# Key loading in 768-byte pieces and key turning by half-width identity products, in a fused attention and feed-forward kernel

## The chip, the cores and the metric

The kernel runs on one core of one Trainium2 chip (trn2). The metric is the device time of one execution in microseconds (us), as the median of several runs. Engine names: PE is TensorE's matrix product, PEld its weight load, ACT is ScalarE, DVE is VectorE, POOL is GpSimd, SP is SyncE, which here only issues DMAs. ACTq and SPq are the instruction queues of ACT and SP, where DMAs are issued.

## The reference

Attention with mixed heads, then a feed-forward layer. Batch 4, 12 heads, 448 positions, head size 64; the feed-forward sizes are 768 and 2048.

```python
scores = scale * np.matmul(q, k.transpose(0, 1, 3, 2))
scores = np.einsum('bhij,hg->bgij', scores, w_pre)
scores = scores - np.max(scores, axis=-1, keepdims=True)
attn = np.exp(scores)
attn = attn / (np.sum(attn, axis=-1, keepdims=True) + 1e-09)
attn = np.einsum('bhij,hg->bgij', attn, w_post)
attn_out = np.matmul(attn, v)
x = attn_out.transpose(0, 2, 1, 3).reshape(B * S, H * D)
h = x @ w_in
g = np.where(h >= 1, h, np.where(h <= -1, 0.0, (h + 1) ** 2 / 4))
return g @ w_out
```

## The kernel before, in words

The program has two halves. The first (about the first 465 us) is the attention, the second the feed-forward layer; only the attention is touched.

The attention goes through 16 tiles of query rows, four for each element of the batch (120, 120, 120 and 88 rows), all 12 heads at once. Each tile is cut into 3 groups, 48 groups in all, and each group holds 3 or 4 blocks: a block has up to 10 query rows times 12 heads, 120 partitions by 448 key positions.

Heads go in pairs, six pairs to an element of the batch. For a pair the keys must lie with the head dimension on the partitions: two heads of 64 fill 128 partitions. `load_k` (L101) brings the keys of a pair into SBUF with the key positions on the partitions; `trans_k` (L136) turns them on PE. Of the 448 positions of a head, 384 go as three blocks of 128 (L141), the last 64 by a product of their own (`rest`, L149). ACT copies the turned keys out of PSUM as the high part (L145), DVE makes the low part (L146). `trans_q` (L153) does the same for the queries of a tile, in two halves of three pairs (L161, L165, L166). `scores` (L169) takes two pairs: three products for each head (high by high, high by low, low by high, L180), copies out by DVE (L185 or L187) and ACT (L189) into `ssb`. With `ring` false the first pair lies in one wide PSUM tile, which DVE copies at once (L187); with `ring` true in two tiles of the ring of six banks `ps_l`, copied one by one (L185). In both cases ACT copies the two heads of the second pair.

Both `load_k` and the tile it fills put the two heads of a pair side by side, so one transpose turns both:

```python
x = x.rearrange("p (r s d) -> p r s d", s=2, d=D)
for s in range(2):
    e.dma_start(out=x[:, :, s, :], in_=k[b, 2 * hp + s, :SM].rearrange("(p r) d -> p r d", r=KC))
```

In DRAM the three rows `r` of a partition are 768 contiguous bytes; in the tile they lie apart, so the transfer moves pieces of 256 bytes.

From `ssb` each block is fetched again by DMA with rows and heads on the partitions (`load_s`, L202, tile `s`), mixed over heads on PE (`pre`, L221 and L223), maximum on DVE (L226), exponential on ACT (L232), the second mix on PE (`post`, L260, and `post_rest`, L276), and the product with the values on PE (`pv`, L306 and L311). `post` and `pv` write 64 PSUM partitions at a time: products with 64 columns of weights that go to one or the other column half of PE, two at once.

The order is written by hand (`manual_schedule`): every engine works through its instructions in program order, and a waiting instruction holds what stands behind it. The main loop (L893) issues for group n, on PE: `pre` of its blocks, the turning of the next element's keys and of the next tile's queries where they are due, `pv`, `post_rest` and `post` of the group before, then `scores` of the next tile. The keys of the next element are turned in three consecutive groups, two pairs in each, so in 9 groups over the whole program; they are fetched one group earlier. DMA issues go through the queues of SP and, for some keys of the first tile, of ACT. Completion semaphores are used in turn, so a DMA's issue can also wait until the DMA that had its semaphore before has landed.

The first tile has code of its own (L758 to L823). It loads the queries (L762, L767, L770) and the first element's keys (L766 to L769) into three tiles `k0`, which later become those of the values; builds the identity on POOL; issues products of the identity with itself, whose result nobody reads (`warm`, L788), so that PE has work while the first data come; turns queries and keys, makes the scores in three steps of two pairs, loads the values, fetches the first blocks, and goes on to the second tile's scores.

Of the kernel before, what the change touches and what calls it, by code (L numbers as in the profile page):

```python
# [22 lines left out]
def tile_talking_heads_moe(  # L23
# [76 lines left out]

    def load_k(b, hp, t=None):  # L101
        e = nc.scalar if t is not None and hp > 2 else nc.sync
        if t is None:
            t = qp.tile([128, 2 * S // 128 * D + D], F32, tag="kraw", name="kraw", bufs=2)
            x, y = t[:, :2 * KC * D], t[:KR, 2 * KC * D:]
            i = ident[:KR, :KR]
        else:
            j = hp % 2
            x, y = t[:, 2 * KC * D * j:2 * KC * D * (j + 1)], t[j * KR:(j + 1) * KR, 4 * KC * D:]
            i = ident[j * KR:(j + 1) * KR, j * KR:(j + 1) * KR]  # L110
        x = x.rearrange("p (r s d) -> p r s d", s=2, d=D)
        y = y.rearrange("p (s d) -> p s d", d=D)
        for s in range(2):
            e.dma_start(out=x[:, :, s, :], in_=k[b, 2 * hp + s, :SM].rearrange("(p r) d -> p r d", r=KC))
        e.dma_start(out=y, in_=k[b, 2 * hp:2 * hp + 2, SM:].rearrange("s p d -> p s d"))
        kraw[b, hp] = x, y, i

# [8 lines left out]
    def load_v(b, g):  # L126
        t = ap_.tile([128, 4 * KC * D + 2 * D], F32, tag=f"v{g}", name=f"v{g}", bufs=1)
        x = t[:, :4 * KC * D].rearrange("p (h c) -> p h c", h=4)
        y = t[:, 4 * KC * D:].rearrange("p (s d) -> p s d", d=D)
        nc.sync.dma_start(out=x, in_=v[b, 4 * g:4 * g + 4, :SM].rearrange("h (p r) d -> p h (r d)", r=KC))  # L130
        for m in range(2):
            h = 4 * g + 2 * m
            nc.sync.dma_start(out=y[half[m]], in_=v[b, h:h + 2, SM:].rearrange("s p d -> p s d"))
        vt[b, g] = x, y

    def trans_k(b, hp):  # L136
        kt[b, hp] = [qp.tile([128, S], F32R, tag=f"k{c}{hp}", name=f"k{c}{hp}", bufs=1) for c in "hl"]
        x, y, i = kraw.pop((b, hp))
        ps = ps_l.tile([128, S], F32, tag="l", name="ps_k")
        for r in range(KC):  # L140
            nc.tensor.transpose(out=ps[:, r * 128:(r + 1) * 128], in_=x[:, r, :, :], identity=ident)  # L141

        def out():
            hi, lo = kt[b, hp]
            nc.scalar.activation(out=hi, in_=ps, func=AF.Copy)  # L145
            nc.vector.tensor_tensor(out=lo, in0=ps, in1=hi.bitcast(F32), op=ALU.subtract)  # L146

        def rest():
            nc.tensor.transpose(out=ps[:, SM:], in_=y, identity=i)  # L149
            return out  # L150
        return rest
# [17 lines left out]
    def scores(t, hps, ring=False):  # L169
# [13 lines left out]
        if ring:  # L183
            for s in range(2):
                nc.vector.tensor_copy(out=ssb[t][:n, h + s, :], in_=ps[0][s][:n])  # L185
        else:
            nc.vector.tensor_copy(out=ssb[t][:n, h:h + 2, :], in_=wide[:n, :, :S])  # L187
        for s in range(2):
            nc.scalar.activation(out=ssb[t][:n, 2 * hps[1] + s, :], in_=ps[1][s][:n], func=AF.Copy)  # L189

# [567 lines left out]
    with tc.manual_schedule():  # L758
# [6 lines left out]
        ident = qp.tile([128, 128], F32, name="ident", bufs=1)  # L765
        load_k(0, 0, k0[0])  # L766
        load_q(0, (1,))  # L767
        for hp in range(1, HP):
            load_k(0, hp, k0[hp // 2])  # L769
        load_q(1)  # L770
# [18 lines left out]

        warm(12)  # L790
        trans_q(0, 0)()()
        trans_k(0, 0)()()
        warm(3)
        trans_q(0, 1)()()
        warm(4)
        trans_k(0, 1)()()
        for g in range(3):
            scores(0, [2 * g, 2 * g + 1], g == 1)
            if g < 2:
# [311 lines left out]
```

## Time and profile before

| what | value |
|---|---|
| median of 3 runs | 873.71 us (872.88 to 875.06) |
| profiled execution, its own time | 873.89 us |
| its span, first to last instruction | 872.2 us |
| PE busy | 855.1 us, 98% of the span |
| DVE, ACT, POOL busy | 644.0, 563.0, 212.7 us |
| mean granted clock of PE | 0.998 |

The span is the stretch that the profile's rows cover; 1.7 us of the execution's own time lie outside it. A row of the timeline gives start, length, engine, line, operation, what it writes and reads, the shape and how many such instructions follow one another. PE's instructions overlap: a single one is in the pipeline for some 270 ns, though the next may start 110 ns later, so the time that a run of them costs is read from start to start. A float32 product stands as two records, a transpose as one. The chain of waits is followed back from the last instruction to whatever released it.

### The profile page before, as it was taken

How to read it: one execution, taken by the hardware profiler on the slowest of the kernel's cores; microseconds unless marked ns; L12 is line 12 of the kernel's file. 1: busy time of each engine (PE TensorE's matmuls, PEld its weight loads, DVE VectorE, ACT ScalarE, POOL GpSimd, SP SyncE). 2: the span in 40 equal slices, each digit the busy share in tenths (PEclk: the TensorE clock that was granted, in tenths of full speed). 3: DMA queues.
4: the chain of work that ended last, by engine and by line, in shares of the span. 5: the costliest groups of instructions: out<-in, count | busy, mean ns of one | idle time of the engine just before them, and what ended most of it. 6: DMA issues, size and time to landing. Idle time of an engine off the chain costs nothing.

```text
span 872.2 us, 19952 instructions
## 1 busy us (share of the span) xinstructions
PE 855.1 (98%) x7848; PEld 735.8 (84%) x7848; DVE 644.0 (74%) x938; ACT 563.0 (65%) x1171; POOL 212.7 (24%) x269
## 2 busy tenths in 40 slices
PE   8999999999999999999999999999999999999998
PEld 6678777777777787777778788899999999999998
DVE  3887587775767866768578977997668978777853
ACT  3788788787877777778666466676667434433431
POOL 0366245662455633656320000000000000000000
PEclk9999999999999999999999999999999999999999
DMA  7887769987689875997556755664434544123331
GB/s 161 238 250 216 220 192 258 276 238 217 180 248 263 252 212 154 277 269 254 189 171 171 250 180 175 208 188 128 127 109 163 174 153 136 55 90 111 108 128 63
DMA packets 155329, 162.47 MB, mean 186 GB/s; under 512 B 66916, under 2 KB 148964, under 8 KB 155236
## 3 DMA queue, kind: packets, MB, share of 16 engines
q1 hardware_dynamic: 152404, 160.51, 61.1%
q8 instruction: 62, 1.02, 0.5%
q10 hardware_dynamic: 2832, 0.69, 0.4%
q14 instruction: 31, 0.25, 0.1%
HBM read 88.81 MB, written 33.82 MB: 141 GB/s over the span
## 4 chain that ended last, share of the span: by engine, by line
PE 83%; DMA 6%; DVE 4%; ACT 4%; SPq 2%; issue 1%; POOL 0%; ACTq 0%; DVEq 0%; POOLq 0%
PE ps_f L712 23%; PE ps_f L547 21%; PE ps_a L260 10%; PE ps_l L223 7%; DMA s<-ssb 5%; PE ps_q L311 5%; PE ps_l L221 4%; PE ps_q L180 3%; PE ps_s L180 3%; PE ps_r L276 2%; PE ps_q L306 1%; ACT e L232 1%; PE ps_t L161 1%; SPq L202 1%; PE ps_k L141 1%
## 5 line engine op out<-in xcount | busy, mean ns | idle before, releaser
L243 POOL TENSOR_SCALAR wr<-wpost,rs 120x120 f32<-120x120 f32 x180 | 140.3, 795 | 62.5 <-DVE rs L239 43.2
L232 ACT ACTIVATE e<-ps_l,nm 120x448 f32<-120x448 f32 x180 | 112.2, 631 | 63.1 <-DVE nm L226 61.8
L260 PE MATMUL ps_a<-wr,e 120*64 120x120 f32 (+1 forms) x2160 | 118.9, 266 | 0.0
L226 DVE TENSOR_REDUCE nm<-ps_l 120x1 f32<-120x448 f32 x180 | 105.0, 617 | 14.3 <-PE ps_l L223 10.8
L260 PEld LDWEIGHTS ps_a<-wr,e 120*64 120x64 f32 x2160 | 110.2, 137 | 2.6 <-issue 2.6
L695 ACT ACTIVATE sgh_p<-gq_p 128x1024 fp32r<-128x1024 f32 (+1 forms) x56 | 53.3, 953 | 89.9 <-PE ps_f L712 89.7
L223 PE MATMUL ps_l<-s,wpre 120*120 120x448 f32 x196 | 94.8, 568 | 5.7 <-DMA s<-ssb 3.4
L439 DVE SCALAR_TENSOR_TENSOR wl<-wi,wh 128x768 fp32r<-128x768 f32 x71 | 67.7, 953 | 41.9 <-ACT wh L436 41.9
L712 PE MATMUL ps_f<-wh,sgh_p 128*128 128x384 f32 x294 | 98.2, 334 | 0.0
L712 PE MATMUL ps_f<-wh,sgl_p 128*128 128x384 f32 x294 | 98.2, 334 | 0.0
L712 PE MATMUL ps_f<-wl,sgh_p 128*128 128x384 f32 x294 | 98.2, 334 | 0.0
L436 ACT ACTIVATE wh<-wi 128x768 fp32r<-128x768 f32 x71 | 59.7, 842 | 58.0 <-DVE wi L659 18.0
L262 ACT ACTIVATE aT<-ps_a 128x360 f32<-128x360 f32 x180 | 79.4, 498 | 12.9 <-PE ps_a L260 4.7
L696 DVE TENSOR_TENSOR sgl_p<-gq_p,sgh_p 128x1024 fp32r<-128x1024 f32 (+1 forms) x56 | 60.8, 1088 | 35.8 <-ACT sgh_p L695 35.8
L210 DVE CAST sh<-s 120x448 fp32r<-120x448 f32 (+1 forms) x82 | 32.9, 401 | 59.2 <-DMA s<-ssb 59.0
L187 DVE COPY ssb<-ps_q 120x896 f32<-120x896 f32 (+1 forms) x46 | 49.9, 1084 | 26.9 <-PE ps_q L180 26.8
L189 ACT ACTIVATE ssb<-ps_s 120x448 f32<-120x448 f32 (+1 forms) x96 | 47.5, 554 | 20.7 <-PE ps_s L180 17.6
L377 POOL TENSOR_TENSOR wt<-wt,wk 128x768 int32<-128x768 int32 x32 | 58.2, 1820 | 8.9 <-ACT wk L373 5.8
L221 PE MATMUL ps_l<-sh,wpre_h 120*120 120x448 f32 (+1 forms) x82 | 59.6, 726 | 0.0
L712 PEld LDWEIGHTS ps_f<-wh,sgh_p 128*128 128x128 f32 x294 | 55.2, 188 | 0.0
L712 PEld LDWEIGHTS ps_f<-wl,sgh_p 128*128 128x128 f32 x294 | 55.2, 188 | 0.0
L712 PEld LDWEIGHTS ps_f<-wh,sgl_p 128*128 128x128 f32 x294 | 55.2, 188 | 0.0
(235 smaller groups left out, 1949.4 us busy)
## 6 DMA issues: line engine op xcount, KB each, us to landing
s<-ssb SPq DMA_DIRECT2D x172, 210.0 KB
wraw<-in_moe_w_in_dram SPq DMA_DIRECT2D x16, 768.0 KB
wraw<-in_moe_w_out_dram SPq DMA_DIRECT2D x16, 768.0 KB
wi<-wod SPq DMA_DIRECT2D x29, 384.0 KB
wi<-wsd SPq DMA_DIRECT2D x28, 384.0 KB
wsd<-wt SPq DMA_DIRECT2D x16, 384.0 KB
wod<-wt SPq DMA_DIRECT2D x16, 384.0 KB
wi<-wss SPq DMA_DIRECT2D x16, 384.0 KB
```

The source lines that it names most:

```text
L221: nc.tensor.matmul(out=lps[m], lhsT=w[:k], rhs=y[:k], start=(j == 0), stop=(j == 2))
L223: nc.tensor.matmul(out=lps[m], lhsT=wpre[:k], rhs=x[:k], start=True, stop=True)
L226: nc.vector.tensor_reduce(out=nm, in_=lps[m], axis=AX.X, op=ALU.max, negate=True)
L232: nc.scalar.activation(out=e, in_=ps, func=AF.Exp, bias=nm, accum_out=sm[:, j:j + 1])
L243: nc.gpsimd.tensor_scalar_mul(out=w[:, :, :ni], in0=wpost[:, :, :ni], scalar1=rs[:, j:j + 1])
L260: nc.tensor.matmul(out=ps[half[s], r, :ni * H], lhsT=e[:, c0:c0 + 64], rhs=w[:, :, :ni], start=True, stop=True)
L262: nc.scalar.activation(out=a[:, :, :, c:c + ni], in_=ps[:, :, :ni * H].rearrange("q r (h i) -> q r h i", h=H), func=AF.Copy)
L436: nc.scalar.activation(out=hi, in_=t, func=AF.Copy, scale=2.0 ** -8)
L439: nc.vector.scalar_tensor_tensor(out=lo, in0=t, scalar=2.0 ** -8, in1=hi.bitcast(F32), op0=ALU.mult, op1=ALU.subtract)
L547: nc.tensor.matmul(out=o, lhsT=u[:, c, k], rhs=x, start=first and r == 0 and m == 0, stop=r == 2 and m == 2, skip_group_check=True)
L696: nc.vector.tensor_tensor(out=lo, in0=src, in1=hi.bitcast(F32), op=ALU.subtract)
L712: nc.tensor.matmul(out=o, lhsT=x[:, f, c], rhs=y[:, f % 2, :], start=first and f == 0 and m == 0, stop=hf == 1 and f == 3 and m == 2, skip ...
```

## The change

The keys of a pair, or of four heads in the first tile, are now loaded by one DMA whose pieces are 768 bytes, with the heads one after the other in the tile. A 128-column block of weights with both heads is then no longer contiguous, and `trans_k` makes two products of 64 columns with the identity instead of one transpose, one for each head, into the two partition halves of PSUM. In the first tile the loads are regrouped (one DMA for four heads; the 64-position rests of the first four pairs on ACT's queue, all else on SP's), there are 8 of the unread products instead of 19, the second pair's keys are turned before the second half of the queries, and all steps but the first use the ring. In ring steps DVE now copies the first head of both pairs and ACT the second head of both.

```diff
-    def load_k(b, hp, t=None):
-        e = nc.scalar if t is not None and hp > 2 else nc.sync
...
-        x = x.rearrange("p (r s d) -> p r s d", s=2, d=D)
-        y = y.rearrange("p (s d) -> p s d", d=D)
-        for s in range(2):
-            e.dma_start(out=x[:, :, s, :], in_=k[b, 2 * hp + s, :SM].rearrange("(p r) d -> p r d", r=KC))
-        e.dma_start(out=y, in_=k[b, 2 * hp:2 * hp + 2, SM:].rearrange("s p d -> p s d"))
-        kraw[b, hp] = x, y, i
+    def load_k(b, hp):
+        t = qp.tile([128, 2 * KC * D + 2 * D], F32, tag="kraw", name="kraw", bufs=2)
+        load_rows(k, nc.sync, t[:, :2 * KC * D], b, 2 * hp, 2)
+        y = load_rest(k, nc.sync, t[:KR, 2 * KC * D:], b, 2 * hp)
+        kraw[b, hp] = t[:, :2 * KC * D].rearrange("p (s r d) -> p s r d", s=2, d=D), y, ident[:KR, :KR]
+
+    def load_rows(x, e, t, b, h, n):
+        e.dma_start(out=t.rearrange("p (h c) -> p h c", h=n),
+                    in_=x[b, h:h + n, :SM].rearrange("h (p r) d -> p h (r d)", r=KC))
+
+    def load_rest(x, e, t, b, h):
+        y = t.rearrange("p (s d) -> p s d", d=D)
+        e.dma_start(out=y, in_=x[b, h:h + 2, SM:].rearrange("s p d -> p s d"))
+        return y
+
+    def load_k0(g, part, e):
+        t = k0[g]
+        if part == 0:
+            load_rows(k, e, t[:, :4 * KC * D], 0, 4 * g, 4)
+            return
+        j = part - 1
+        y = load_rest(k, e, t[half[j], 4 * KC * D:], 0, 4 * g + 2 * j)
+        x = t[:, :4 * KC * D].rearrange("p (h r d) -> p h r d", h=4, d=D)
+        kraw[0, 2 * g + j] = x[:, 2 * j:2 * j + 2], y, ident[half[j], half[j]]
...
         for r in range(KC):
-            nc.tensor.transpose(out=ps[:, r * 128:(r + 1) * 128], in_=x[:, r, :, :], identity=ident)
+            for s in range(2):
+                nc.tensor.matmul(out=ps[half[s], r * 128:(r + 1) * 128], lhsT=x[:, s, r, :], rhs=ident,
+                                 start=True, stop=True)
...
         if ring:
-            for s in range(2):
-                nc.vector.tensor_copy(out=ssb[t][:n, h + s, :], in_=ps[0][s][:n])
+            for u in range(2):
+                nc.vector.tensor_copy(out=ssb[t][:n, h + 2 * u, :], in_=ps[u][0][:n])
...
         for s in range(2):
-            nc.scalar.activation(out=ssb[t][:n, 2 * hps[1] + s, :], in_=ps[1][s][:n], func=AF.Copy)
+            u, i = (s, 1) if ring else (1, s)
+            nc.scalar.activation(out=ssb[t][:n, 2 * hps[u] + i, :], in_=ps[u][i][:n], func=AF.Copy)
...
-        load_k(0, 0, k0[0])
+        load_k0(0, 0, nc.sync)
+        for g in range(2):
+            for part in (1, 2):
+                load_k0(g, part, nc.scalar)
         load_q(0, (1,))
-        for hp in range(1, HP):
-            load_k(0, hp, k0[hp // 2])
+        for g in (1, 2):
+            load_k0(g, 0, nc.sync)
+        for part in (1, 2):
+            load_k0(2, part, nc.sync)
         load_q(1)
...
-        warm(12)
+        warm(7)
         trans_q(0, 0)()()
+        warm(1)
         trans_k(0, 0)()()
-        warm(3)
+        trans_k(0, 1)()()
         trans_q(0, 1)()()
-        warm(4)
-        trans_k(0, 1)()()
         for g in range(3):
-            scores(0, [2 * g, 2 * g + 1], g == 1)
+            scores(0, [2 * g, 2 * g + 1], g > 0)
```

`load_v` uses the two new helpers and issues the same transfers as before. The line numbers below of the changed program differ from those of the program before by 7 to 14.

On PE, at the start of the program, before (`ps_q<-ident` are the unread products, `k_91` the keys of the first four heads, `kh` and `kl` the high and low parts):

```order
L788 MATMUL ps_q<-ident 128x128 x12
L161 MATMUL ps_t<-ident,qraw 128x120 x3
L141 MATMUL ps_k<-ident,k_91 128x128 x3
L149 MATMUL ps_k<-ident,k_91 128x64
L788 MATMUL ps_q<-ident 128x128 x3
L161 MATMUL ps_t<-ident,qraw 128x120 x3
L788 MATMUL ps_q<-ident 128x128 x4
L141 MATMUL ps_k<-ident,k_91 128x128 x3
L149 MATMUL ps_k<-ident,k_91 128x64
L180 MATMUL ps_q<-kh_149,qh 120x448 x2
```

and in the changed program:

```order
L802 MATMUL ps_q<-ident 128x128 x7
L169 MATMUL ps_t<-ident,qraw 128x120 x3
L802 MATMUL ps_q<-ident 128x128
L148 MATMUL ps_k<-ident,k_91 64x128 x6
L157 MATMUL ps_k<-ident,k_91 128x64
L148 MATMUL ps_k<-ident,k_91 64x128 x6
L157 MATMUL ps_k<-ident,k_91 128x64
L169 MATMUL ps_t<-ident,qraw 128x120 x3
L188 MATMUL ps_q<-kh_136,qh 120x448 x2
```

Eleven unread products are gone, each three transposes have become six half-width products, and the second half of the queries comes last.

On SP's queue, at the start of the program, before (`k_92`, `k_93` are the keys of heads 4 to 7 and 8 to 11; ACT's queue held nine more DMAs of keys, six of 128x3x64 and three of 64x2x64):

```order
L124 DMA qraw<-in_q_dram 120x6x64
L114 DMA k_91<-in_k_dram 128x3x64 x2
L115 DMA k_91<-in_k_dram 64x2x64
L124 DMA qraw<-in_q_dram 120x6x64
L114 DMA k_91<-in_k_dram 128x3x64 x2
L115 DMA k_91<-in_k_dram 64x2x64
L114 DMA k_92<-in_k_dram 128x3x64 x2
L115 DMA k_92<-in_k_dram 64x2x64
```

and in the changed program, where ACT's queue holds four DMAs of 64x2x64:

```order
L132 DMA qraw<-in_q_dram 120x6x64
L108 DMA k_91<-in_k_dram 128x4x192
L132 DMA qraw<-in_q_dram 120x6x64
L108 DMA k_92<-in_k_dram 128x4x192
L108 DMA k_93<-in_k_dram 128x4x192
L113 DMA k_93<-in_k_dram 64x2x64 x2
```

Twelve transfers of 128x3x64 have become three of 128x4x192.

On PE, in the first of the 9 groups that turn keys in the main loop, as a difference of the stretch (the lines around are renumbered only):

```order
-L141 MATMUL ps_k<-ident,kraw 128x128 x6
-L161 MATMUL ps_t<-ident,qraw 128x120 x3
-L149 MATMUL ps_k<-ident,kraw 128x64 x2
+L148 MATMUL ps_k<-ident,kraw 64x128 x12
+L169 MATMUL ps_t<-ident,qraw 128x120 x3
+L157 MATMUL ps_k<-ident,kraw 128x64 x2
```

Six transposes have become twelve half-width products; what stands before and behind them stays.

## Rows read from the trace of the kernel before

**Rows 1.** The page: busy time of PE; the chain that ended last, by engine.

```profile
PE 855.1 (98%) x7848; PEld 735.8 (84%) x7848; DVE 644.0 (74%) x938; ACT 563.0 (65%) x1171; POOL 212.7 (24%) x269
...
PE 83%; DMA 6%; DVE 4%; ACT 4%; SPq 2%; issue 1%; POOL 0%; ACTq 0%; DVEq 0%; POOLq 0%
```

**Rows 2.** Busy time of each engine by stretch, granted clock, DMA share, GB/s.

```profile
0.00:24.00 24.00, 21.20 (x135) 16.12 (x136) 10.87 (x22) 9.82 (x21) 1.12 (x9) 1.00 0.71 169
77.90:107.70 29.80, 29.80 (x383) 24.01 (x381) 19.72 (x36) 21.34 (x55) 11.81 (x18) 1.00 0.74 216
188.20:218.00 29.80, 29.80 (x384) 24.05 (x382) 19.23 (x35) 21.85 (x55) 11.80 (x18) 1.00 0.75 216
301.30:331.00 29.70, 29.70 (x383) 23.98 (x381) 19.35 (x35) 21.49 (x54) 11.21 (x18) 1.00 0.79 219
137.00:165.00 28.00, 26.37 (x338) 20.53 (x336) 20.65 (x38) 20.65 (x56) 16.62 (x17) 1.00 0.92 272
230.00:275.00 45.00, 42.12 (x534) 32.59 (x531) 31.82 (x59) 34.22 (x86) 24.16 (x27) 0.96 0.89 259
345.00:390.00 45.00, 41.92 (x543) 32.70 (x539) 33.46 (x59) 33.52 (x89) 25.38 (x27) 1.00 0.91 270
```

**Rows 3.** The chain in order of time, in a group that turns keys: start, length, what.

```profile
80.29 0.61 PE ps_l L221 x3
80.90 0.66 PE ps_k L141 x6
...
84.42 2.46 PE ps_a L260 x48
```

**Rows 4.** Line 141 alone: the key transposes of the main loop.

```profile
L141 PE MATMUL ps_k<-ident,kraw x54: 270/272/274, 80.7 to 324.5; 128*128 128x128 f32 x54
```

**Rows 5.** Timeline of PE: full-width products followed by half-width ones.

```profile
126.10 0.37 PE L221 MATMUL ps_l<-sh,wpre_l 120*120 120x448 f32 x1
126.31 0.37 PE L221 MATMUL ps_l<-sl,wpre_h 120*120 120x448 f32 x1
126.61 0.43 PE L306 MATMUL ps_q<-aR,v 64*64 64x120 f32 x8
```

**Rows 6.** Timeline of PE, first tile.

```profile
1.41 5.49 PE L788 MATMUL ps_q<-ident 128*128 128x128 f32 x24 [1.41 <-POOL mask L778]
6.69 0.68 PE L161 MATMUL ps_t<-ident,qraw 120*128 120x120 f32 x3
...
8.92 1.06 PE L788 MATMUL ps_q<-ident 128*128 128x128 f32 x8
9.82 0.49 PE L141 MATMUL ps_k<-ident,k 128*128 128x128 f32 x3
...
10.76 0.46 PE L180 MATMUL ps_q<-kh,qh 64*120 64x448 f32 x2 [0.25 <-ACT kh L145]
...
12.79 0.55 PE L141 MATMUL ps_k<-ident,k 128*128 128x128 f32 x3
...
13.47 0.55 PE L141 MATMUL ps_k<-ident,k 128*128 128x128 f32 x3
...
16.03 0.55 PE L141 MATMUL ps_k<-ident,k 128*128 128x128 f32 x3
```

**Rows 7.** The chain in order of time, first tile.

```profile
3.38 3.98 DMA qraw<-in_q_dram
...
9.81 0.47 ACT qh L165
...
19.38 0.97 ACT ssb L189 x2
```

**Rows 8.** Timeline, first tile: DMA issues on ACT's queue, ACT's first use of data.

```profile
9.12 0.63 ACTq L115 DMA_DIRECT2D k<-in_k_dram  x1
9.80 0.47 ACT L165 ACTIVATE qh<-ps_t 128x360 fp32r<-128x360 f32 x1 [7.52 <-DMA k<-in_k_dram]
```

**Rows 9.** The DMA queue's own waits, whole span: in total, times, longest.

```profile
SPq L202 <- DVE ssb L187: 60.3, 13, 10.4
```

More of the change, by code (lines that the diff above doesn't have):

```diff
@@ L99, in pair @@
         return ps_q.tile([128, 2, 512], F32, tag="q", name="ps_q")
-    def load_k(b, hp, t=None):
-        e = nc.scalar if t is not None and hp > 2 else nc.sync
[L103 to L110, printed above, removed]
-        x = x.rearrange("p (r s d) -> p r s d", s=2, d=D)
-        y = y.rearrange("p (s d) -> p s d", d=D)
-        for s in range(2):
-            e.dma_start(out=x[:, :, s, :], in_=k[b, 2 * hp + s, :SM].rearrange("(p r) d -> p r d", r=KC))
-        e.dma_start(out=y, in_=k[b, 2 * hp:2 * hp + 2, SM:].rearrange("s p d -> p s d"))
-        kraw[b, hp] = x, y, i
+    def load_k(b, hp):
[19 more added lines that the diff above has]
+        kraw[0, 2 * g + j] = x[:, 2 * j:2 * j + 2], y, ident[half[j], half[j]]
     def load_q(t, gs=(0, 1)):
@@ L127, in load_v @@
         t = ap_.tile([128, 4 * KC * D + 2 * D], F32, tag=f"v{g}", name=f"v{g}", bufs=1)
-        x = t[:, :4 * KC * D].rearrange("p (h c) -> p h c", h=4)
-        y = t[:, 4 * KC * D:].rearrange("p (s d) -> p s d", d=D)
-        nc.sync.dma_start(out=x, in_=v[b, 4 * g:4 * g + 4, :SM].rearrange("h (p r) d -> p h (r d)", r=KC))
+        load_rows(v, nc.sync, t[:, :4 * KC * D], b, 4 * g, 4)
         for m in range(2):
-            h = 4 * g + 2 * m
-            nc.sync.dma_start(out=y[half[m]], in_=v[b, h:h + 2, SM:].rearrange("s p d -> p s d"))
-        vt[b, g] = x, y
+            load_rest(v, nc.sync, t[half[m], 4 * KC * D:], b, 4 * g + 2 * m)
+        vt[b, g] = (t[:, :4 * KC * D].rearrange("p (h c) -> p h c", h=4),
+                    t[:, 4 * KC * D:].rearrange("p (s d) -> p s d", d=D))
     def trans_k(b, hp):
```

## The prediction

> **What bounds the kernel now.** I read the page first. PE is busy for 98% of the span and makes up 83% of the chain that ended last [rows 1]. Such an average says little about one stage, so I then asked for busy times by stretch [rows 2]. The three stretches in which keys are turned in the main loop (78 to 108, 188 to 218, 301 to 331 us) show PE busy for all of their 29.8, 29.8 and 29.7 us, while the DMA engines are busy for 74 to 79%. The chain confirms it: from one product to the next, with the key transposes (L141) as a link of their own [rows 3]. There the kernel is bound by PE's throughput, and a transfer that lands earlier has nobody waiting for it. PE stands idle in other places: 2.8 us in the first 24 us, and 1.6, 2.9 and 3.1 us where the next element of the batch begins (137 to 165, 230 to 275, 345 to 390 us), with the DMA engines at 89 to 92% [rows 2]. In the first tile the chain is not PE's: it runs through the landing of queries and keys until 9.81 us and then through copies, mostly ACT's [rows 7].
>
> So the change has two parts that must be priced apart: what it does to PE in the nine key-turning groups, and what it does to the first 24 us.
>
> **Keys in the main loop: PE.** Of 54 transposes [rows 4], three to a pair, 18 pairs, every one becomes two products of 64 columns.
> - A transpose costs 0.11 us: six stand as 0.66 us in the chain [rows 3].
> - A float32 product of the same 128 moving columns costs twice that. Four unread products run from 8.92 to 9.82 us, 0.225 us each [rows 6].
> - Two half-width products with different column halves run side by side. In `post`, 48 records, 24 products of 120 columns, take 2.46 us in the chain [rows 3]: 0.205 us for two, which is 0.22 us at 128 columns. That is the price of one full-width product.
>
> So three transposes at 0.33 us become three pairs of products at 0.66 us: 0.33 us more for each pair of heads, 5.9 us for 18.
>
> Changing between full-width and half-width products costs something too. Between two products of one kind start-to-start is 0.21 us (126.10 to 126.31); before the first half-width one it is 0.30 us [rows 5], 0.09 us more. The changed program switches twice more in each group (into the half-width products, and back for the query transposes): 0.18 us for 9 groups, 1.6 us. That row also changes the number of rows used, so it is the nearest I have and not the same case: zero is the other end. I take it whole, since a switch is a switch of the array's use either way.
>
> Main loop: 7.5 us longer, bounds 5.9 and 7.5. Nothing covers it, PE having no idle time there [rows 2].
>
> A rule speaks against the change more strongly than the rows do. The Trainium skill ("TensorE: Matmul & The Clock Gate", Terms) calls transpose mode four times faster for float32; by that a pair of heads would go from 0.33 to 1.31 us and the main loop would lose 17.6 us and the switches. The trace disagrees: 0.225 against 0.11 us is a factor of two, and I go by it. The Trainium skill ("TensorEngine Tiling (Array Packing)", Key Properties) also says that changing the tiling mode drains TensorE; the 0.09 us above agrees with it, and by that rule the 1.6 us stand.
>
> **Keys in the main loop: DMA.** Each group issues two DMAs fewer, some 0.6 us each on SP's queue, and the key pieces are three times as large. I cost this at nothing gained: PE waits for no transfer in those stretches. Nor does the earlier queue help the later element boundaries, since SP has idled meanwhile: its block fetches waited 60.3 us in total for DVE's copies, once for 10.4 us [rows 9]. The fetches, value loads and copies behind the boundaries are all released by PE's work and move with it. If that cover went, the saved issue time would be worth at most 18 times 0.6 us, 11 us; I see no place where it is.
>
> **The first tile.** Before, ACT's queue issued nine DMAs, each of the later ones held until an older one had landed. The last issue stood at 9.12 us, so ACT's first copy came at 9.80 us, 7.5 us late, and the chain goes through it [rows 7, 8]. Now ACT issues four rests at about 0.63 us [rows 8], free by 3.5 us.
> - The four heads' keys are issued second on SP, at about 1.3 us. A transfer of queries in the crowded queue took 3.98 us from issue to landing [rows 7]; with that the keys land at 5.3 us. I allow 5.3 to 6.
> - PE: twelve unread products took 1.41 to 6.69 us, 0.44 us each [rows 6], at half the speed of the later ones, though the granted clock stands at 1.00 for the stretch [rows 2]. By their length they ran at 1.2 GHz of the two levels, and PE had only just begun to work. Seven end at about 4.5, the query transposes at 5.1, the eighth at 5.6. The first pair's keys, three pairs of products at 0.44 us and the rest, are turned by 7.1 us, the second's by 8.0 to 8.6, the other queries by 8.4 to 9.0. ACT and DVE keep pace behind. Scores can begin at 8.5 to 9, against 10.76 before [rows 6], and find both pairs ready: 1.4 us instead of 2.0. At the point where the third pair's keys are turned, 12.79 us before [rows 6], 2.2 to 3.0 us are gained.
> - Each of the next two steps took 3.24 us (12.79 to 16.03) [rows 6]. Turning a pair takes 0.68 us there (12.79 to 13.47), now 1.01, and PE has to turn two before the scores: 0.66 us more, less the waits on ACT and DVE that this covers. I put 0.1 to 0.45 us on each step, 0.2 to 0.9 in all.
> - After the last step ACT copied two heads, 0.97 us [rows 7]; now ACT and DVE copy one each: 0.4 us gained before the block fetches can start.
>
> Sum: 1.7 to 3.2 us earlier, 2.5 us taken. The unread products that are gone are no gain of their own: they filled waiting time.
>
> **Sum.** The profiled execution took 873.9 us by itself; minus 2.5 plus 7.5 gives 878.9. It lay 0.2 us above the median of the runs shown, so I predict 878.7 us, 0.6% slower. About 0.3% (2.6 us) is what a measurement here can tell from no change: 871.1 to 876.3 counts as the same.
>
> **The rivals.**
> - *As worked out, slower:* with the bounds of both parts 876.4 (5.9 less 3.2) to 879.5 (7.5 less 1.7), and up to 881 with chance in the waits at the boundaries. Chance 0.60.
> - *No difference that can be told:* no cost for switching, the first tile at its better end, and the stretch with a granted clock of 0.96 in 45 us [rows 2] happens not to recur (3.4 us at half the clock, 1.7 us of PE's work). 876.4 less 1.7 is 874.7. For it: PE's pause before that dip may fall differently in any run. Against: it needs all three. Chance 0.20.
> - *Not slower:* the element boundaries give back what the key groups cost. PE idles for 7.6 us in the three boundary stretches [rows 2]; if those waits end with a stream of transfers that does not move when PE falls behind, PE's extra 7.5 us are paid out of them and only the first tile shows: 871.2, or 870.5 at its better end. It decides if more than some 5 us of the 7.6 come back. For it: DMA share near 0.9 there. Against: SP's waits for DVE's copies [rows 9], by which the stream is tied to PE. Chance 0.11.
> - *The halves do not run side by side,* or PE takes them one after another because each pair alternates strictly: 1.31 us for three pairs of products instead of 0.66, 0.65 us more for 18 pairs, 11.8 us on top, 890. The skill's factor of four would come out in the same place. Against: `post` reads the same moving data for both halves, and reaches 0.205 us [rows 3]. Chance 0.04.
> - *The first tile gives nothing,* because the four heads' DMA lands after 8 us or PE, with fewer unread products, stays at 1.2 GHz longer: 881.2. Chance 0.05.
>
> **How the numbers follow.** The point is the first case. Slower by over 0.3% takes the first and the last two: 0.69; the same 0.20; faster 0.11. The range 873.5 to 881.5 holds the first case, the second and most of the fifth, about 8 in 10; the first case's own range is 876.4 to 881.
>
> **What would show it.** In the profile after, six key products of a pair should stand as 12 records in some 0.66 us; a key-turning group should be longer by 0.75 to 0.85 us, nine times, with PE still without idle time; the first product of `pre` should start some 2.5 us earlier than before; ACT's first copy before 6 us. Wrong would be: key-turning groups of unchanged length, smaller idle time of PE at the boundaries with the same end, or a first copy by ACT that still waits until 9 us.

## The result and the profile after

The changed kernel takes 881.28 us (median of 11 runs, 877.09 to 886.01), the kernel before in the same job 874.13 us (11 runs): a ratio of 1.0083, 95% interval 1.0059 to 1.0106, or 7.2 us more. 878.7 was forecast, with 873.5 to 881.5 as the range: slower, as said, and by 2.2 us more than the sum of +5.0. The profiled execution took 884.64 us by itself (span 882.9), 3.4 us above its median. That matters below.

The page after, busy time of PE and the chain by engine, answers [rows 1]: PE's busy time grew by 9.2 us (stretches at the half clock count in it), and its share of the chain from 83 to 85%.

```profile
PE 864.3 (98%) x8042; PEld 741.4 (84%) x8042; DVE 648.3 (73%) x939; ACT 569.2 (64%) x1171; POOL 214.3 (24%) x269
...
PE 85%; DMA 7%; SPq 3%; DVE 3%; ACT 2%; issue 1%; ACTq 0%; DVEq 0%
```

The three key-turning stretches of [rows 2] after, each from the first `pre` product of the first key group to that behind the third (columns: stretch, length, busy PE, PEld, DVE, ACT and POOL, granted clock, DMA share, GB/s):

```profile
77.72:110.19 32.47, 32.47 (x437) 25.68 (x435) 19.77 (x35) 21.89 (x55) 11.06 (x18) 1.00 0.76 211
191.42:223.90 32.48, 32.48 (x438) 25.68 (x436) 19.52 (x35) 21.88 (x54) 11.00 (x18) 1.00 0.65 198
308.53:340.99 32.46, 32.46 (x437) 25.69 (x435) 19.06 (x34) 22.02 (x55) 9.92 (x17) 1.00 0.71 210
```

Before, between the same two `pre` products, the first three key groups lasted 29.8 us:

```profile
77.91:107.74 29.83, 29.83 (x383) 24.00 (x381) 19.75 (x36) 21.33 (x55) 11.80 (x18) 1.00 0.74 216
```

Now they last 32.5, PE busy throughout. PE's timeline in one of them, after, the place of [rows 3]:

```profile
80.34 0.37 PE L230 MATMUL ps_l<-sl,wpre_h 120*120 120x448 f32 x1
80.64 1.53 PE L148 MATMUL ps_k<-ident,kraw 128*64 128x128 f32 x24
82.10 0.53 PE L169 MATMUL ps_t<-ident,qraw 120*128 120x120 f32 x3
82.56 0.33 PE L157 MATMUL ps_k<-ident,kraw 64*128 64x64 f32 x2
82.82 0.44 PE L315 MATMUL ps_q<-aR,v 64*64 64x120 f32 x8
```

From the last `pre` product to the first of `pv` it is 2.48 us (82.82 less 80.34). And the same place before, which the rows ahead of the prediction don't show in one view:

```profile
80.53 0.37 PE L221 MATMUL ps_l<-sl,wpre_h 120*120 120x448 f32 x1
80.74 0.82 PE L141 MATMUL ps_k<-ident,kraw 128*128 128x128 f32 x6
81.42 0.53 PE L161 MATMUL ps_t<-ident,qraw 120*128 120x120 f32 x3
81.87 0.34 PE L149 MATMUL ps_k<-ident,kraw 64*128 64x64 f32 x2
82.14 0.44 PE L306 MATMUL ps_q<-aR,v 64*64 64x120 f32 x8
```

1.61 us then, so +0.87. Entering the half-width products takes 0.30 us after the last `pre` product instead of 0.21 (+0.09). The twelve half-width products and the way out take 1.46 us (82.10 less 80.64) instead of 0.68 (+0.78).

PE's timeline of the first tile after, for [rows 6]:

```profile
1.41 3.36 PE L802 MATMUL ps_q<-ident 128*128 128x128 f32 x14 [1.41 <-POOL mask L792]
4.56 0.81 PE L169 MATMUL ps_t<-ident,qraw 120*128 120x120 f32 x3
...
6.58 1.55 PE L148 MATMUL ps_k<-ident,k 128*64 128x128 f32 x12 [0.78 <-DMA k<-in_k_dram]
...
8.36 1.55 PE L148 MATMUL ps_k<-ident,k 128*64 128x128 f32 x12
...
10.62 0.47 PE L188 MATMUL ps_q<-kh,qh 64*120 64x448 f32 x2
...
12.04 0.88 PE L148 MATMUL ps_k<-ident,k 128*64 128x128 f32 x12
...
15.82 0.88 PE L148 MATMUL ps_k<-ident,k 128*64 128x128 f32 x12
...
23.69 3.27 PE L232 MATMUL ps_l<-s,wpre 120*120 120x448 f32 x8
```

PE ran out of work at 5.81 us and waited 0.78 us for the keys. The same twelve records then took 1.55 us twice and 0.88 us later: by their length half speed, 1.2 GHz of the two levels. The stretch's own row in the view by stretch shows a granted clock of 1.00 all the same, since that view counts time without a clock record as 1.00; the first record of this trace, of the full clock, stands at 10.25 us. The row:

```profile
5.81:10.20 4.39, 3.62 (x27) 2.72 (x28) 1.16 (x2) 0.61 (x2) 0.00 (x0) 1.00 0.93 231
```

ACT's part went as forecast. Its first copy, at 9.80 us in [rows 8], in ACT's timeline after:

```profile
5.40 0.47 ACT L173 ACTIVATE qh<-ps_t 128x360 fp32r<-128x360 f32 x1 [3.12 <-PE ps_t L169]
```

Yet the first `pre` product starts at 23.69 us, before at 23.77: nothing is gained where 2.5 us were forecast. Before:

```profile
23.77 3.27 PE L223 MATMUL ps_l<-s,wpre 120*120 120x448 f32 x8
```

By the start of the last group this execution is 10.2 us behind that of before. Where they lie, by the start of the first `pre` product of each group after less before (my differences of PE's timelines):

| stretch | after less before, us |
|---|---|
| to the first `pre` product | -0.08 |
| groups 0 to 6 | -0.11 |
| three key groups, three times | +2.64, +2.72, +2.70 |
| what lies between them, with the element boundaries, and the last groups | +0.75, +1.35, +0.26 |

The nine key groups make 8.06 us, 0.90 each. The boundaries make 2.4: PE's waits between 140 and 440 us come to 9.4 us, before to 8.1, and there are two stretches of 3.4 us at the half clock (granted clock 0.50) instead of one. Such a stretch is 1.65 us of lost work: the group with the first of them lasts 10.85 us, before, at the full clock, 9.20.

### The profile page after: what moved, and what is told of

Read it like the earlier page. It is cut to its first block, busy times and chain, and to the rows that moved or that the text cites. A ratio compares the mean times of both kernels' runs of the same rounds, so it can differ in the third digit from the quotient of the medians.

```text
span 882.9 us, 20310 instructions
## 1 busy us (share of the span) xinstructions
PE 864.3 (98%) x8042; PEld 741.4 (84%) x8042; DVE 648.3 (73%) x939; ACT 569.2 (64%) x1171; POOL 214.3 (24%) x269
## 4 chain that ended last, share of the span: by engine, by line
PE 85%; DMA 7%; SPq 3%; DVE 3%; ACT 2%; issue 1%; ACTq 0%; DVEq 0%
PE ps_f L721 23%; PE ps_f L556 21%; PE ps_a L269 10%; PE ps_l L232 8%; PE ps_q L320 5%; PE ps_l L230 5%; DMA s<-ssb 5%; PE ps_q L188 3%; PE ps_s L188 3%; PE ps_k L148 2%; PE ps_r L285 2%; SPq L211 1%; PE ps_q L315 1%; DMA v<-in_v_dram 1%; PE ps_t L169 1%
## 5 line engine op out<-in xcount | busy, mean ns | idle before, releaser
L235 DVE TENSOR_REDUCE nm<-ps_l 120x1 f32<-120x448 f32 x180 | 106.9, 620 | 17.6 <-PE ps_l L232 13.2
L271 ACT ACTIVATE aT<-ps_a 128x360 f32<-128x360 f32 x180 | 81.5, 492 | 16.1 <-PE ps_a L269 5.2
L247 POOL TENSOR_SCALAR rs<-sm 120x4 f32<-120x4 f32 (+1 forms) x48 | 14.4, 301 | 182.0 <-ACT e L241 182.0
```

The lines of the kernel that those rows point to most:

```text
L235: nc.vector.tensor_reduce(out=nm, in_=lps[m], axis=AX.X, op=ALU.max, negate=True)
L271: nc.scalar.activation(out=a[:, :, :, c:c + ni], in_=ps[:, :, :ni * H].rearrange("q r (h i) -> q r h i", h=H), func=AF.Copy)
```

## The experiments

The kernel before stood beside each set, with medians of 873.3 to 874.3 us. Theory at first: the key groups cost 8 us and nothing gives it back; the first tile's gain was lost to the late keys and the half clock.

**1. The two parts apart.** The loop alone: the first tile is that of before.

```diff
+        if b:
+            e.dma_start(out=x.rearrange("p (h c) -> p h c", h=2),
+                        in_=k[b, 2 * hp:2 * hp + 2, :SM].rearrange("h (p r) d -> p h (r d)", r=KC))
...
+            for s in range(2):
+                nc.tensor.matmul(out=ps[half[s], r * 128:(r + 1) * 128], lhsT=x[:, s, r, :], rhs=ident,
```

> The first tile as before; keys of elements 1 to 3 loaded in 768 B pieces and turned by half-width products. Theory (the products cost PE time that nothing covers, the first tile of the change neither gains nor loses): nine key-turning groups longer by 0.80 to 0.96 us each, 7.9 us in all, 881 to 883 us, the same as the whole change. Rival (part of the loss comes from the first tile or what it shifts): clearly less than the whole change, some 878. Rival (the loop costs nothing and the first tile is the cause): 874.

881.57 us (6 runs), ratio 1.0092 (1.0059 to 1.0125), +8.0 us by the ratio. The three key groups of an element grow by 0.88 to 0.96, 0.96 and 0.80 us, 8.1 us for all nine. The whole loss is in the loop.

The first tile alone: the changed kernel, with the loop of before.

```diff
-        load_rows(k, nc.sync, t[:, :2 * KC * D], b, 2 * hp, 2)
+        for s in range(2):
+            nc.sync.dma_start(out=x[:, :, s, :], in_=k[b, 2 * hp + s, :SM].rearrange("(p r) d -> p r d", r=KC))
...
+            if b:
+                nc.tensor.transpose(out=ps[:, r * 128:(r + 1) * 128], in_=x[:, r, :, :], identity=ident)
+                continue
```

> The first tile as changed; keys of elements 1 to 3 as before, with transposes. Theory: no gain in the first tile, 873.5 to 874.5 us, the first product of the first mix at 23.7 us after the start where PE's clock rises late (10 us), about 2 us sooner where it rises by 6 us. Rival (the first tile of the change is itself slower): 876 or more. Rival (it gains, and the profiled execution was an unlucky one): 871.5.

873.26 us (12 runs), ratio 0.998 (0.9956 to 1.0004): not told from no change. In its trace, though, the first `pre` product starts 2.23 us earlier. PE's timeline:

```profile
6.01 0.88 PE L153 MATMUL ps_k<-ident,k 128*64 128x128 f32 x12 [0.29 <-DMA k<-in_k_dram]
...
21.54 3.27 PE L237 MATMUL ps_l<-s,wpre 120*120 120x448 f32 x8
```

So the mechanism works where the keys are early and PE is at full speed, and what it gives is not all there at the end: by the last group the 2.23 us are 1.43.

**2. Filling PE's wait.** The same with more unread products.

```diff
-        warm(1)
+        warm(6)
```

> As the run with the changed first tile alone, but six unread products instead of one stand before the first keys, so that PE does not fall idle while it waits for them (0.78 us of idle time in the profile after). Theory (PE stayed at 1.2 GHz because of that idle time): PE's clock rises by 8.3 us at the latest, turning the second pair takes 1.0 us instead of 1.8, the scores begin at about 9.5 instead of 10.6 us, and the execution is 0.5 to 1 us shorter. Rival (landing of keys and the products themselves set the pace): no difference.

875.67 us (12 runs), ratio 1.0019 (0.9997 to 1.004). Missed: the products overshot. PE's timeline shows the key products behind them at 7.69 us, at full speed, while the keys had landed at 6.24:

```profile
5.15 2.61 PE L807 MATMUL ps_q<-ident 128*128 128x128 f32 x12
7.69 0.88 PE L153 MATMUL ps_k<-ident,k 128*64 128x128 f32 x12
```

**3. A short first tile with the transposes kept.** Before, with all its key loads on SP, the second pair ahead of the other queries, the copies shared and seven unread products fewer.

```diff
-        e = nc.scalar if t is not None and hp > 2 else nc.sync
+        e = nc.sync
...
-        warm(3)
-        trans_q(0, 1)()()
-        warm(4)
         trans_k(0, 1)()()
+        trans_q(0, 1)()()
```

> The kernel before with transposes and 256 B pieces everywhere, but all key loads of the first tile on SP's queue (ACT issues none), the second pair's keys loaded and turned before the second half of the queries, twelve unread products, and the copies by ring as in the change. Theory (of the change's first tile only freeing ACT and sharing out the copies pays, products on halves cost): scores begin near 9 us, steps of 3.0 us, the first mix starts at some 21 us, 871 to 872 us, faster than both kernels. Rival (256 B pieces on one queue land too late): scores begin no earlier than 10.7 us, and the time is that of before.

876.97 us (12 runs), ratio 1.0038 (1.0015 to 1.006): slower, and both readings missed. The scores began at 9.19 us instead of 10.76, but SP's queue became the bound. It reaches the first score fetches at 23.32 us, where before it did so at 20.38, and PE waits 4.41 us for them. SP's queue here, then before, then PE here:

```profile
21.96 1.25 SPq L133 DMA_DIRECT2D v<-in_v_dram  x2
23.32 4.99 SPq L203 DMA_DIRECT2D s<-ssb  x6
...
20.38 5.81 SPq L202 DMA_DIRECT2D s<-ssb  x7
...
26.27 1.96 PE L224 MATMUL ps_l<-s,wpre 120*120 120x448 f32 x3 [4.41 <-DMA s<-ssb]
```

**4. The keys of the first tile in two transfers.** Experiment 1's second kernel, the first transfer halved.

```diff
-            load_rows(k, e, t[:, :4 * KC * D], 0, 4 * g, 4)
+            w = 2 if g == 0 else 4
+            for h in range(0, 4, w):
+                load_rows(k, e, t[:, h * KC * D:(h + w) * KC * D], 0, 4 * g + h, w)
```

> The changed first tile with the loop of before, and the keys of the first four heads in two transfers of two heads (768 B pieces) in place of one of four. Theory (in the changed first tile TensorE ran out of work before the keys were there, 0.29 us in one run and 0.78 us in another, and in the second the clock was then granted at 10.25 us only, so that all the first steps ran at half speed): a transfer of half the size lands by about 5.3, before the one unread product ends at 5.7 to 5.8; no idle time ahead of the key products, the clock granted by 7, key products of the first pair 0.88 to 1.2 us, scores from 8.0 to 8.8, first pre product at 21.2 to 21.9 (before 23.77), and the time 1.5 to 3 us under before. Rival (when the clock is granted is chance, whatever TensorE did before): the clock may be granted as late as 10 us without any idle time ahead of it, first pre product near 23.7, the time as before.

874.01 us (12 runs), ratio 1.0002 (0.9983 to 1.0022). PE's timeline did what theory said: no wait ahead of the keys, and the first `pre` product 2.63 us earlier than before.

```profile
5.60 0.88 PE L155 MATMUL ps_k<-ident,k 128*64 128x128 f32 x12
...
21.14 3.27 PE L239 MATMUL ps_l<-s,wpre 120*120 120x448 f32 x8
```

The time did not follow. Ahead of the first element boundary the lead is still 2.8 us, behind it 0.3; 1.6 of the 2.5 us went in a stretch at the half clock (159.0 to 162.4 us, granted clock 0.50) behind a wait of 1.84 us for fetched scores. And the changed kernel again, for a second profile:

> The changed kernel once more, for its first tile. Theory (the start depends on when the keys land and when the clock is granted): where the clock is granted by 7.5 us the scores start at 8.4 to 9.2 and the first pre product at 21.4 to 22.2, and where it is granted at 10 or later the numbers of the first look come again (10.6 and 23.7); the key groups cost 0.80 to 0.96 us each in both cases. Rival (the first tile of the changed kernel gains nothing at any time): first pre product at 23.5 to 23.8 with the clock granted early.

884.27 us (one run). The keys came at 6.90 us, after a wait longer than in the first profile, and yet PE ran them at full speed:

```profile
6.90 0.88 PE L148 MATMUL ps_k<-ident,k 128*64 128x128 f32 x12 [1.10 <-DMA k<-in_k_dram]
...
22.44 3.27 PE L232 MATMUL ps_l<-s,wpre 120*120 120x448 f32 x8
```

Four runs line up: from the first key product to the first `pre` product it is 15.53 or 15.54 us (5.60 to 21.14, 6.01 to 21.54, 6.90 to 22.44, 7.69 to 23.23). Every microsecond by which the keys are late is one at the end of the first tile, and the half clock comes on top: 17.11 in the first profile. Does the wait for the keys hold up the full clock? This run is no test: the first clock record of its trace, of the full clock, stands at 5.80 us, just as the wait began. The 14 profiles speak for it: the full clock came at 5.41 to 7.45 us in the nine without such a wait, at 5.51 to 5.80 in the three where it was there when the wait began, and at 10.25 and 14.37 in the two where PE ran out of work at 5.8 us without it (the first profile, and that of experiment 5, with a wait of 0.66). No run changes the wait alone and nothing else, so the cause is read from the traces and not shown.

**5. What the switch costs.** The changed kernel, with the queries and rests ahead of the halves, so that the halves stand next to those of `pv`.

```diff
-                        at.setdefault(w0, []).insert(hp % 2, lambda nb=nb, hp=hp: trans_k(nb, hp))
+                        at.setdefault(w0, []).append(lambda nb=nb, hp=hp: trans_k(nb, hp))
...
+        rest()
+        def halves():
```

> The changed kernel, with one edit in the loop: in a group that turns keys the queries and the last 64 positions come first and the products on column halves of both pairs last, right ahead of the column-half products of the output (pv). So TensorE goes from full width to column halves once there instead of twice. Theory (each going in and out costs about 0.2 us, beside 0.66 us for the twelve pairs of products that are too many): each of the nine key groups gains 0.15 to 0.25 us, its start shifts by 0.65 to 0.75 over before instead of 0.80 to 0.96, and the time is 1.5 to 2 us under the changed kernel's. Rival (the loss is the products alone, the time between the groups of products is the same wherever they stand): the shifts stay at 0.80 to 0.96 and the time is the changed kernel's within 0.5 us. Second rival: the copies of queries and keys come later or in another order on ScalarE, and the scores wait for them: the same shifts, with idle time ahead of the scores.

880.76 us (7 runs), ratio to before 1.0081 (1.0052 to 1.011): the total doesn't tell it from the changed kernel, where 1.5 to 2 us were expected. PE's timeline does:

```profile
82.32 0.37 PE L242 MATMUL ps_l<-sl,wpre_h 120*120 120x448 f32 x1
82.53 0.47 PE L181 MATMUL ps_t<-ident,qraw 120*128 120x120 f32 x3
82.93 0.34 PE L159 MATMUL ps_k<-ident,kraw 64*128 64x64 f32 x2
83.19 1.53 PE L168 MATMUL ps_k<-ident,kraw 128*64 128x128 f32 x24
84.65 0.44 PE L327 MATMUL ps_q<-aR,v 64*64 64x120 f32 x8
```

2.33 us from the last `pre` product to `pv`, 0.15 less than 2.48. The first two groups of the first three grow by 0.73 and 0.80 us instead of 0.88 and 0.96, a gain of 0.15 and 0.16; so do those of the other elements. The third, which turns no queries ahead of its rests, stays at 0.81: its rests, full width but on 64 rows, start 0.85 us behind the last `pre` row of the timeline, the halves of the changed kernel 0.84 and the transposes of before 0.75. So going over to 64 rows costs what going over to column halves costs. One way in and out costs 0.15 us where it can be saved; of the 0.73 us that are left, 0.66 are the products.

**6. The loads alone.** Before, with the loop's keys in pieces of 768 B and three full-width products per pair on the columns as they lie. The heads and rows of the keys then come out in the wrong order; this kernel leaves out putting them right, and is there for its time alone.

```diff
+            y0 = x.rearrange("p s r d -> p (s r d)")[:, r * 128:(r + 1) * 128]
+            nc.tensor.transpose(out=ps[:, r * 128:(r + 1) * 128], in_=y0, identity=ident)
```

> Before, with the keys of the loop loaded in pieces of 768 B, but turned by six... three products of full width per pair as before, on the columns as they lie: the rows of the key matrix come out in another order and under the wrong heads, which this kernel leaves so. Theory (in the loop the loads lie beside other work and one transfer less per pair frees nothing): each group starts within 0.1 us of before, and the time is before's within 1 us. Rival (larger pieces free the queue or the transfers, and the changed kernel's loss is the sum of that gain and a larger loss): 1 to 4 us under before.

875.22 us (10 runs), ratio 1.0019 (0.9996 to 1.0042); eight of the nine key groups have before's length to 0.02 us, one is 0.24 longer. In this order of the work the larger pieces give nothing.

**7. Why the start's gain is lost.** In experiment 4's kernel PE waited for fetched scores at the boundaries. Waits of PE from 140 to 400 us there (in total, times, longest):

```profile
PE ps_l L239 <- DMA s<-ssb: 6.8, 4, 2.1
PE ps_s L195 <- DVE ql L181: 2.5, 2, 1.6
```

Two theories: the fetches stand behind the value loads on SP, or the DMA engines are full. First, the value loads of elements 1 to 3 issued by GpSimd:

```diff
-        load_rows(v, nc.sync, t[:, :4 * KC * D], b, 4 * g, 4)
+        e = nc.gpsimd if b else nc.sync
+        load_rows(v, e, t[:, :4 * KC * D], b, 4 * g, 4)
```

> The run with the keys of the first four heads in two transfers and the loop of before, with one edit: the value loads of elements 1 to 3 are issued by GpSimd in place of SP. In that run the start was 2.6 us earlier and the time was before's: at each element boundary TensorE waited 1.8 to 2.1 us for fetched scores ahead of a pre product, and a stretch of 3.4 us at the half clock came behind two of the three waits. Theory (the score fetches stand on SP behind the value loads, which take 3 to 5.7 us of that queue there): the fetches are issued up to 2 us earlier, each of the three waits falls under 1 us, at most one stretch of the half clock is left, 869 to 872 us. Rival (the 16 DMA engines are at 0.92 to 1.0 of their time in these stretches, and the order of issue changes nothing): the same waits of about 2 us and 873 to 875 us.

874.36 us (10 runs), ratio 1.0003 (0.9981 to 1.0025). The single waits became shorter (1.0 to 1.6 us) and more; the time stayed, so the place of the value loads on SP's queue is not what sets it. Then the weight conversions kept out of the boundaries and put into the key groups:

```diff
-    CS = [n for n in range(2, NG - 5) if not any(x <= n < x + 3 for x in (3 * t - 5 for t, y in enumerate(tiles)
+    CS = [n for n in range(2, NG - 5) if not any(x <= n < x + 3 for x in (3 * t + 1 for t, y in enumerate(tiles)
```

> The same run with another single edit: the weight conversions (a load, a store, work on three engines) leave out the three groups of 14 that lie around an element boundary (3t+1 to 3t+3) in place of the three key groups, so that their transfers don't meet the value loads. Theory (the DMA engines' traffic sets the waits at the boundaries): the three waits of 1.8 to 2.1 us fall under 1 us, and 869 to 872 us come out if the key groups bear the conversions; they may grow by up to 0.3 us each (9 groups, 2.7 us), which would take it back to 874. Rival (the queue's order sets the waits): waits as they were, and the key groups longer: 874 to 877 us.

870.59 us (8 runs), ratio 0.9956 (0.9932 to 0.998): faster than both kernels. The boundary stretches of [rows 2] in its view by stretch: PE busy for all of them, the DMA share at 0.70 to 0.74 instead of 0.89 to 0.92.

```profile
137.00:165.00 28.00, 28.00 (x368) 22.04 (x367) 20.40 (x37) 20.14 (x57) 11.77 (x18) 1.00 0.70 218
230.00:275.00 45.00, 45.00 (x585) 35.23 (x583) 33.37 (x60) 35.04 (x91) 20.40 (x27) 1.00 0.74 234
345.00:390.00 45.00, 45.00 (x599) 35.78 (x595) 34.05 (x62) 34.85 (x92) 22.86 (x30) 1.00 0.74 232
```

This edit moves the conversions' transfers, but their issues on SP and their work on three engines too. The landings tell these apart: from its issue to its landing a score fetch of the three stretches took 7.0, 7.8 and 7.6 us in experiment 4's kernel (medians of the trace's records), 8.2 to 8.6 with the values on GpSimd's queue, and 3.6 to 3.8 here. So the transfers themselves were slow, and the traffic theory holds. The key groups pay 9.5 us for it, more than the 2.7 expected, much of it in one wait of 3.5 us and the half clock behind it; the boundaries give back more. So what of the 3.7 us is the start's, and what does this order do to the change itself? Before and the changed kernel, each with this one edit:

> Before, with its own first tile and loop, and the weight conversions moved away from the element boundaries as in the run that came out at 870.59 us. Theory (with the waits at the boundaries gone, what the start gains stays to the end, so that run owes 2.0 us of its 3.7 to the start): 872 to 873.5 us, the first pre product at 23.4 to 23.8, no wait of TensorE of over 0.5 us between 137 and 400 us except in key groups. Rival (the whole gain is from the boundaries and the start still counts for nothing): 870 to 871.3 us.

874.16 us (12 runs), ratio 0.9997 (0.9971 to 1.0022). Both readings missed: the waits at the boundaries are gone, but `post` waits in the key groups. PE's waits from 24 to 400 us:

```profile
PE ps_a L260 <- DVE kl L146: 9.8, 7, 2.0
```

What of the 3.7 us is the start's stays open: this kernel's first `pre` product stands 1.9 us behind that of the run of 870.59 us, but its key groups lose more too (12.8 us against 9.5).

> The changed kernel, first tile and loop, with the weight conversions moved away from the element boundaries. Theory (the 8 us of the key groups are TensorE's own work and stay, and the waits at the boundaries, some 8 us and the half-clock stretches behind them, go as they did with the loop of before): 3 to 5 us under the changed kernel, 876 to 878.5 us, and 5 to 7 us over the run of 870.59 us. Rival (in the key groups the conversions now meet work that is longer by 0.9 us each, so that GpSimd's and VectorE's waits there are covered by it, and a part of the 8 us comes back): 872 to 875 us.

870.78 us (12 runs), ratio 0.9966 (0.9943 to 0.999): 10.5 us under the changed kernel by the medians of two jobs, the rival and more. Against before with the same edit, in the same job, it is 3.4 us less (868.83 to 874.58 against 872.41 to 877.63 us). Its key groups, by stretch, are as long as the changed kernel's to 0.01 us, with the conversions inside them:

```profile
78.30:110.77 32.47, 32.47 (x437) 25.67 (x435) 23.40 (x40) 26.48 (x60) 15.87 (x19) 1.00 0.91 269
```

Before's, with the conversions, took 34.95 us, PE busy for 30.43:

```profile
77.85:112.80 34.95, 30.43 (x383) 24.00 (x381) 22.37 (x40) 25.25 (x61) 16.17 (x19) 1.00 0.90 244
```

The waits of VectorE in these two stretches show the difference; first that of the changed kernel with the edit, then that of before with it:

```profile
DVE sh L219 <- DMA s<-ssb: 3.4, 3, 1.3
```

```profile
DVE sh L210 <- DMA s<-ssb: 11.6, 3, 4.1
```

VectorE takes the keys' low parts (kl) behind the split of fetched scores. With small pieces SP spends 5.6 us issuing one group's key loads (71.32 to 76.96) and with large ones 3.6 (72.05 to 75.67), and the fetches follow them. The first and last of these issues, before with the edit, then the changed kernel with it:

```profile
71.32 2.02 SPq L114 DMA_DIRECT2D kraw<-in_k_dram  x2
...
76.33 0.63 SPq L115 DMA_DIRECT2D kraw<-in_k_dram  x1
...
72.05 0.70 SPq L108 DMA_DIRECT2D kraw<-in_k_dram  x1
...
75.04 0.63 SPq L113 DMA_DIRECT2D kraw<-in_k_dram  x1
```

So in this order the DMA part of the change seems to be worth something, and the longer products to cover what is left. That, and the split between the two, is read from the traces; no run takes them apart.

## Why the prediction was right, and which step failed

- *Main loop, +7.5 us: right, but 8.06 in the trace lies above its upper bound of 7.5.* By the loop alone it is +8.0. The 0.66 us of products per group stand as forecast. The term that was too small is the switches: put at 0.18 us per group, they make 0.21 of the 0.87 in the group shown and 0.15 to 0.30 elsewhere, 2.1 us over the nine groups (8.06 less 5.94) instead of 1.6. The Trainium skill ("TensorEngine Tiling (Array Packing)", Key Properties) says that a change of tiling mode drains TensorE, and gives no price. These 0.15 to 0.30 us per group are what the changes cost here. Halves run side by side: the rival of 890 is out.
- *DMA in the loop, nothing: right,* by the loads alone. The cover named for it was PE's full load, and when conversions stood in the key groups and PE waited there, the saving seems to have counted.
- *Boundaries give back nothing: right.* They took 2.4 us more in the first profile. But the reason given, that the transfers move with PE, holds in one direction only: an early start is lost there in part or nearly whole (2.8 us became 0.3 at the first boundary in experiment 4's kernel, 2.2 became 1.4 by the last group in experiment 1's second), since the transfers are at their limit.
- *First tile, -2.5 us: this step failed.* At the third pair's keys, 2.2 to 3.0 us of gain were put (2.4 to 2.9 by its own terms); 0.75 were there in the first profile (12.04 against 12.79 us) and 2.01 in the second. Keys put at 5.3 to 6 us were used at 6.58 and 6.90. The first pair was put at half speed, and the second at 0.9 to 1.5 us; in the first profile both ran at half speed, and the second took 1.77. The steps behind took 3.78 us (12.04 to 15.82), 0.54 more than 3.24, where 0.1 to 0.45 was put. The 0.4 us behind the last step came (from the query transposes to the next scores 1.10 us instead of 1.50). That adds up to -0.08 in the first profile and -1.33 in the second. The mechanism was right: with the keys at 5.60 the sum is -2.63. But the forecast added a start's gain to an end that had other waits in between, and that was wrong too: 2.2 and 2.6 us gained at the first `pre` product came to -1.7 and +0.2 us at the end by the ratios, neither told from nothing.
- *The total, in part by luck.* The median of 881.28 lies 0.3 us above the first case's own range, 876.4 to 881, and 0.2 us under the end of the stated one. The rival "the first tile gives nothing" (0.05) has the number, 881.2, but its reasons hold by half: the keys landed at 6.54, not after 8, and the 1.2 GHz lasted longer in one of two profiles; the other gained 1.33 us and took 884.27 all the same.

## What to carry to other kernels

A transpose replaced by float32 products on column halves costs twice the time plus, here, some 0.2 us for each way into the halves and out, and it is paid in full where TensorE is the bound. Before a gain at the start is added to the end, look for the stretches behind it where transfers are at their limit: here they ate part of a lead or nearly all of it. And the same change was +7 us in one order of the side work and, with the weight conversions moved, stood at 870.78 against 874.16 us, 3.4 us less: price a change against the order it will live in, and try moving what fills the limit.

## Unexpected of the hardware

- When the clock comes up after the start varies from run to run of the same first-tile instructions: key products of 0.88 us at 6.90 us in one, of 1.55 us at 6.58 in another. In the run of experiment 5 it came so late, at 14.37 us, that its first `pre` product stood at 25.47 us, 19.0 us behind its first key product instead of 15.5. In both late cases TensorE had paused for under 0.8 us before the full clock was there.
- The four heads' keys came in one transfer of 16 parts, and the last part decides: in the second profile of the changed kernel 15 parts had landed by 5.49 us and the last at 6.86.
- In the main loop each fall to the half clock lasted 3.4 us or twice that, and 17 of the 18 in these profiles stood in or behind a wait of TensorE of 1.8 to 4.4 us (one behind 1.4). Not every such wait was followed by one (1.99 us in experiment 4's kernel, 2.12 in the second profile of the changed kernel, were not). At 1.65 us each these falls are one reason why a single execution strays: the profiled one of the changed kernel lay 3.4 us above its median.
